# Spreading a weight conversion over two stages of a fused attention and mixture-of-experts kernel

## The chip, the cores and the metric

The kernel runs on one core of one Trainium2 chip. The metric is the time of one execution in device microseconds (us); of several runs the median is given. A profiled execution is one more run, with a trace of every engine: TensorE (PE, its weight loads PEld), VectorE (DVE), ScalarE (ACT), GpSimd (POOL) and SyncE (SP), which here issues most of the loads.

## The reference, cut to what matters

Three stages run one after the other on 2 x 768 tokens: attention in clusters (2 batches, 8 heads, 64 wide), a mixture of 8 experts with one expert for each token, and a dense pair of products with a gate between them.

```
def _moe2_ref(x, w_in, w_out):          # x: 1536 x 512, w_in: 512 x 2048, w_out: 2048 x 512
    h = x @ w_in
    sp = np.where(h > 20.0, h, np.log1p(np.exp(np.minimum(h, 20.0))))
    g = h * np.tanh(sp)
    return g @ w_out

def reference(q, k, v, centroids, moe_..., moe2_w_in, moe2_w_out):
    x = _attn_ref(q, k, v, centroids)   # softmax(q k') v within clusters, per head
    x = _moe_ref(x, ...)                # x -> gate * relu(x @ w1[e]) @ w2[e]
    return _moe2_ref(x, moe2_w_in, moe2_w_out)
```

The weights of the last stage arrive as 64-bit floating-point numbers. The change concerns when they are turned into the pairs of 16-bit numbers that the products use.

## The kernel before, in words

Every operand of a product is a pair of f16 tiles, a high part and a low part (the rounding error), and every product is three matmuls (`mm3`: high x high, high x low, low x high).

**Attention.** `attention()` is a generator that yields 3 times for each of 16 heads x 6 key tiles, and the heads' work is written in its slots: scores s (L389), their exponentials e on ACT, eh and el (the low part is a subtraction on POOL, L115), the products av (L425 to L427), row maxima mxh on DVE (L349, L354), the head's output xt (L440). `pregate` and `gate(b)` compute the experts of a batch (gate for batch 0 inside attention, for batch 1 right after it): about 45 small DVE instructions, the last of them L1175, then a scatter of the tokens to a buffer in device memory on POOL (L800), a load of the sorted tokens xs on SP (L830), and sorting products with diagonal tiles dg (L700, L711), whose result is xw.

**Experts.** `moe1()` walks (batch b, slot s, block n): products eps<-xw,w into hT for n < 4, eps<-hT,w into x for n > 3, 24 matmuls of 416 columns a block. Weights come in blocks wf; ACT makes the high part (L916), DVE the low part (L920).

**The last stage.** `h_units(q)` for six pieces q of 256 tokens: 16 products h (f = 0 to 15, L1005 with win, 12 matmuls each). `mish` turns a group of four into activations (ACT with table loads, L1101 to L1111, DVE L1108, POOL L115). `o_units(q)` multiplies them by wout (L1157), in four groups f4.

**The conversion.** `convs("i")` and `convs("o")` convert w_in into win and w_out into wout in 16 chunks each. A chunk is one load raw on SP (L1017, 512 KB, two buffers), three DVE instructions that put the bits of a 64-bit number together as a 32-bit one (L1025, L1026, L1028, all 128x512 into the one tile f), the high part on ACT (L1031) and the low part on DVE (L1033). So it is four DVE instructions a chunk. The generator yields 6 times after the first two loads and 4 times for each chunk, and issues the load of chunk j + 2 after the third DVE instruction of chunk j. Column block j of win is what h for f = j needs; chunk j of wout is row block j.

**What sets the order.** Generators are advanced in turn, and each advance writes instructions. In attention the loop `for na, _ in enumerate(attention())` advances `CI = convs("i")` in every second slot (CI1 = 2) after slot 162 (NA0), except while batch 0's gate is being sorted; whatever is left of CI is written in one go after attention. Then come three calls of `mix`: it always advances the part that has come least far, measured as its progress over the weight that stands beside it. A part that yields None waits for another. The first call mixes slot (0, 1) of the experts, gate 1, 20 steps of the output conversion (CV1) and h_units(0); the second slot (1, 0), h_units(1) and the rest of the output conversion; the third slot (1, 1) and all of the rest. From this program order a scheduler makes the queues of PE, DVE, ACT and POOL, by a model of the times; each engine then works its queue in order. SP's queue stands as it was written.

Of the kernel before, what the change touches and what calls it, by code (L numbers as in the profile page):

```python
# [24 lines left out]
def clustered_attention_moe_kernel(  # L25
# [35 lines left out]
    GAP = 1  # L61
    AVL = 1
    ASK = 2
    CV1 = 20
    FM = 0.35
    SE = 8
    SM = 3
# [10 lines left out]
    F32H = 8  # L78
    WL = 0
    FAST = 1  # L80
    CI1 = 2
    CQ = 0
    WM = 1
    FLD = 0
# [3 lines left out]
    SPK = 1  # L88
    WQ = 2
    BQ = 0  # L90
    GA = 40.0
    NA0 = 3*6*9
    ROW = 2 * DM + 8

# [914 lines left out]
    NF = DF2 // P  # L1009
# [23 lines left out]
        nc.vector.scalar_tensor_tensor(out=dst[:, 1], in0=ff, scalar=64.0, in1=dst[:, 0], op0=ALU.mult, op1=ALU.subtract)  # L1033

    NCV = 16

    def convs(nm):
        n = (DF2 if nm == "i" else NF) // NCV

        def load(j):  # L1040
            if nm == "i":
                conv_load((nm, j), w_in[:, j * n:(j + 1) * n].rearrange("(c p) f -> p c f", p=P), [CD, n])
            else:
                conv_load((nm, j), w_out[j * n * P:(j + 1) * n * P, :].rearrange("(c p) f -> p c f", p=P), [n, DM])

        for j in range(RAWB):
            load(j)
        for _ in range(6):
            yield 1.0
        for j in range(NCV):  # L1050
            if nm == "i":
                ch = conv_chunk((nm, j), win[:, :, :, j * n:(j + 1) * n], [CD, n])
            else:
                ch = conv_chunk((nm, j), m_p["wout"][:, :, j * n:(j + 1) * n, :], [n, DM])
            next(ch)
            yield 1.0
            next(ch)
            yield 1.0
            next(ch)
            if j + RAWB < NCV:  # L1060
                load(j + RAWB)
            yield 1.0
            for _ in ch:
                pass
            yield 1.0

    QW = S // 3
# [48 lines left out]
    o_done = set()  # L1116
# [3 lines left out]
    def h_units(q):  # L1120
        b, p = divmod(q, 3)
        x1 = x1_t[b]
        while (b, min(p, 1)) not in slots_done:
            yield None
        for f in range(NF):
            while q > 1 and (q - 2, f // 4) not in o_done:
                yield None
            if f % FB == 0:
                h_t[q] = m_p["ps"].tile([P, FB, QW], F32, tag="h", name="h", bufs=2)
            mm3(h_t[q][:, f % FB], win, x1[:, :, :, p * QW:(p + 1) * QW], CD, slice(f * P, (f + 1) * P))  # L1130
            advance()
            if f % FB == 1:
                pend.append(mish(h_t[q], gsl[q % 2][f // FB], q, f // FB))
                next(pend[-1])
            h_keys.add((q, f))
            if q > 1:
                yield 1.28
            elif f % 2:
                yield 2.56
# [4 lines left out]
    def o_units(q):  # L1144
        b, p = divmod(q, 3)
        wout = m_p["wout"]
        pts = [m_p["ps"].tile([P, DM], F32, tag="o", name="o", bufs=NQ) for _ in range(NQ)]
        for f4 in range(NF // 4):
            while (q, 4 * f4 + 3) not in g_done:
                if (q, 4 * f4 + 3) in h_keys:  # L1150
                    advance()
                else:
                    yield None
# [105 lines left out]
    def mix(*parts):  # L1259
        for u in gmix(*parts):  # L1260
            assert u is not None
# [12 lines left out]
    CI = convs("i")  # L1274
# [7 lines left out]
    def m_until(b, s):  # L1282
        while (b, s) not in slots_done:
            yield next(M)
# [25 lines left out]
        m_step()  # L1310
    att.close()
    open_second()
    for _ in CI:
        pass

    def gate1():
        while not gs1.done:
# [5 lines left out]

    C1, CH = 33.6, 20.5
    CV = convs("o")
    mix([m_until(0, 1), 2 * C1 - m_done[0]], [gate1(), GA], [part(CV, CV1), float(CV1)], [h_units(0), CH])
    mix([m_until(1, 0), C1], [h_units(1), CH], [CV, 4.0 * NCV + 6 - CV1])
    ho = seq(*[gmix([h_units(q + 2), CH], [o_units(q), CH]) for q in range(4)], o_units(4), o_units(5))
    mix([m_until(1, 1), C1 / FM], [ho, 10 * CH])
    rest()  # L1330


# [33 lines left out]
```

## Time and profile before

| what | us |
|---|---|
| median of 3 runs (708.71 to 711.01) | 709.72 |
| the profiled execution | 704.72 |
| its span, first to last instruction | 703.1 |
| PE busy in the span | 616.4 (88%) |
| DVE busy | 433.1 (62%) |
| ACT busy | 448.4 (64%) |
| POOL busy | 299.1 (43%) |

The shares are averages over stages with different limits. Attention runs to about 326 us (the last xt), batch 1's gate ends at 352 us, the sorted tokens of batch 1 are there at about 387 us, and from 460 us on PE has no gap up to the last products. The conversion's DVE instructions lie between 217.7 and 453.7 us. A busy PE is not PE at its peak, since the ends of matmuls are modelled.

### The profile page before, as it was taken

What the parts mean: (1) busy time and instruction counts of PE and PEld (TensorE: products, weight loads), DVE (VectorE), ACT (ScalarE), POOL (GpSimd) and SP (SyncE); (2) the same over time, 40 slices, a digit from 0 to 9 for tenths busy, and PEclk for the clock granted to TensorE, in tenths of its full rate; (3) what the DMA queues carried; (4) which work ended last, traced back from release to release, by engine and by line L of the source; (5) the groups of instructions that cost most, each with busy time, mean ns of one, the idle gap of its engine ahead of it and who ended that gap; (6) DMA issues with size and microseconds to landing.
All of it is one profiled execution on the core that took longest, in us unless ns stands there. A gap on an engine that the chain in (4) does not pass through costs nothing.

```text
span 703.1 us, 14009 instructions
## 1 busy us (share of the span) xinstructions
PE 616.4 (88%) x5618; PEld 408.3 (58%) x5619; DVE 433.1 (62%) x783; ACT 448.4 (64%) x668; POOL 299.1 (43%) x252
## 2 busy tenths in 40 slices
PE   1698989976678985888999898999999999999995
PEld 1375767744346653554766565666666676667542
DVE  6888888899999999789948888832311101110100
ACT  2587888876457676565597668856645466766500
POOL 5578797995956665542061211111212212313211
PEclk9999999999689999999999999999999999999999
DMA  7532462413833333245545544421100000000000
GB/s 228 139 73 69 111 167 57 106 42 86 277 108 98 97 96 90 79 134 179 151 167 168 176 150 154 147 61 31 46 16 1 7 24 1 31 1 20 12 31 34
DMA packets 56743, 64.43 MB, mean 92 GB/s; under 512 B 10080, under 2 KB 46944, under 8 KB 56672
## 3 DMA queue, kind: packets, MB, share of 16 engines
q1 hardware_dynamic: 42064, 48.74, 24.3%
q10 hardware_dynamic: 12688, 8.42, 3.9%
q0 software_dynamic: 1920, 6.32, 2.3%
q8 instruction: 46, 0.75, 0.4%
q14 instruction: 25, 0.20, 0.1%
HBM read 46.23 MB, written 6.32 MB: 75 GB/s over the span
## 4 chain that ended last, share of the span: by engine, by line
PE 42%; DVE 32%; issue 9%; ACT 6%; DMA 5%; POOL 2%; SPq 1%; POOLq 0%; DVEq 0%; ACTq 0%
PE h L1005 12%; PE o L1157 12%; PE eps L1005 7%; DVE mxh L349 4%; DVE f L1026 4%; DVE w L920 3%; DVE f L1028 2%; DMA QK<-oT 2%; PE s L389 2%; DVE oT L299 2%; DVE mxh L354 2%; DVE f L1025 2%; DVE win L1033 2%; PE x L348 1%; DMA wf<-in_moe_w_dram 1%
## 5 line engine op out<-in xcount | busy, mean ns | idle before, releaser
L115 POOL TENSOR_TENSOR el<-e,eh 128x768 f16<-128x768 f32 x86 | 146.9, 1718 | 59.3 <-ACT eh L398 35.0
L1005 PE MATMUL h<-x,win 128*128 128x256 f16 x1152 | 133.4, 273 | 4.3 <-ACT s L1101 2.8
L1108 DVE SCALAR_TENSOR_TENSOR s<-s,h 128x1024 f32<-128x1024 f32 x24 | 29.3, 1221 | 167.7 <-ACT s L1106 165.1
L1005 PEld LDWEIGHTS <-win 128*128 128x128 f16 x1152 | 112.5, 98 | 24.5 <-issue 5.1
L1005 PEld LDWEIGHTS <-w 128*128 128x128 f16 x768 | 75.1, 99 | 66.9 <-issue 13.5
L115 POOL TENSOR_TENSOR xb<-s,xb 128x1024 f16<-128x1024 f32 x18 | 39.6, 2201 | 142.9 <-ACT xb L1111 142.7
L1157 PE MATMUL o<-wout,xb 128*128 128x512 f16 x432 | 96.8, 379 | 0.0
L391 ACT ACTIVATE e<-s 128x384 f32<-128x384 f32 x152 | 70.2, 486 | 24.7 <-PE s L389 20.1
L389 PE MATMUL s<-QK 128*128 128x384 f16 x320 | 81.9, 347 | 4.4 <-ACT e L391 4.1
L398 ACT ACTIVATE eh<-e 128x768 f16<-128x768 f32 x88 | 73.9, 845 | 16.8 <-PE av L427 7.7
L1005 PE MATMUL eps<-xw,w 128*128 128x416 f16 x384 | 75.1, 344 | 6.2 <-DVE hT L967 3.2
L1005 PE MATMUL eps<-hT,w 128*128 128x416 f16 x384 | 72.7, 342 | 1.4 <-DVE hT L967 1.4
L1101 ACT ACTIVATE s<-h,cst 128x512 f32<-128x512 f32 x48 | 33.0, 687 | 62.6 <-PE h L1005 62.4
L1157 PEld LDWEIGHTS <-xb 128*128 128x128 f16 x432 | 42.3, 98 | 47.6
L425 PE MATMUL av<-vst,eh 128*128 128x65 f16 x528 | 63.9, 197 | 6.8 <-DVE xt L440 5.4
L349 DVE TENSOR_REDUCE mxh<-x 128x1 f32<-128x512 f32 x96 | 63.6, 674 | 5.1 <-PE x L348 4.8
L427 PE MATMUL av<-vst,el 128*128 128x65 f16 x528 | 61.2, 197 | 5.1 <-POOL el L115 4.6
L426 PE MATMUL av<-vst,eh 128*128 128x64 f16 x528 | 64.0, 199 | 0.0
L425 PEld LDWEIGHTS <-eh 128*128 128x128 f16 x528 | 51.1, 100 | 15.8 <-DVE xt L440 8.0
L427 PEld LDWEIGHTS <-el 128*128 128x128 f16 x528 | 51.1, 102 | 11.9 <-POOL el L115 7.1
L426 PEld LDWEIGHTS <-eh 128*128 128x128 f16 x528 | 51.1, 100 | 3.8 <-issue 0.8
L348 PE MATMUL x<-QK 128*128 128x512 f16 x96 | 40.6, 431 | 12.7 <-DVE mxh L349 6.9
(224 smaller groups left out, 1076.7 us busy)
## 6 DMA issues: line engine op xcount, KB each, us to landing
wf<-in_moe_w_dram ACTq DMA_DIRECT2D x16, 512.0 KB, 4.5
raw<-in_moe_w_in_dram SPq DMA_DIRECT2D x16, 512.0 KB, 3.9
raw<-in_moe_w_out_dram SPq DMA_DIRECT2D x16, 512.0 KB, 4.5
wf<-in_moe_w_dram SPq DMA_DIRECT2D x16, 512.0 KB, 3.7
QK<-hl SPq DMA_DIRECT2D x32, 192.0 KB, 3.1
xs<-dr SPq DMA_DIRECT2D x12, 258.0 KB, 3.6
t<-in_k_dram SPq DMA_DIRECT2D x8, 384.0 KB, 4.4
t<-in_q_dram SPq DMA_DIRECT2D x8, 384.0 KB, 3.6
```

What stands on the lines that cost most here:

```text
L115: nc.gpsimd.tensor_tensor(out=out_, in0=in0, in1=in1, op=ALU.subtract)
L348: nc.tensor.matmul(sp, lhsT=st[:, QA, t * P:(t + 1) * P], rhs=st[:, KA, 0:512], start=True, stop=True)
L349: nc.vector.reduce_max(out=mx_t[i][:, t, 0:1], in_=sp, axis=AX.X)
L389: nc.tensor.matmul(sps[hf][:, 0:HS], lhsT=st[:, KA + a, kt * P:(kt + 1) * P], rhs=st[:, QA + a, hf * HS:(hf + 1) * HS], start=(a == 0), st ...
L391: nc.scalar.activation(out=e32[:, hf * HS:(hf + 1) * HS], in_=sps[hf][:, 0:HS], func=AF.Exp, scale=1.0 / float(D) ** 0.5)
L398: nc.scalar.activation(out=eh, in_=e32, func=AF.Copy)
L425: nc.tensor.matmul(av[:, t, :], lhsT=eh[:, cols], rhs=vs[:, h, 0:NV], start=(kt == 0 and t == 0), stop=False, skip_group_check=True)
L426: nc.tensor.matmul(av[:, t, 0:D], lhsT=eh[:, cols], rhs=vs[:, h, NV:], start=False, stop=False, skip_group_check=True)
L427: nc.tensor.matmul(av[:, t, :], lhsT=el[:, cols], rhs=vs[:, h, 0:NV], start=False, stop=(kt == T - 1), skip_group_check=True)
L1005: nc.tensor.matmul(out_, lhsT=wc[:, a, kk, ms], rhs=mv[:, c, kk, :], start=(i == 0), stop=(i == n - 1))
L1101: nc.scalar.activation(out=s[:, u:u + hf], in_=pt[:, u:u + hf], func=AF.Sigmoid, scale=2.0 ** -17, bias=cst[:, 1:2])
L1157: nc.tensor.matmul(pts[t], lhsT=gsl[q % 2][f // FB][:, f % FB, a, t * P:(t + 1) * P], rhs=wout[:, c, f, :], start=(f == 0 and i_ == 0), st ...
```

## The change

Conversion in attention runs in every fourth slot instead of every second (CI1), and what is left of it is no longer written at once: it goes on in the first `mix`, together with the first 26 steps of the output conversion instead of 20. The first two calls of `mix` become one. The rest of the output conversion, so far in the second call, goes into the last one, with a weight of 5 x 64 beside 205 for h and o. A set cv_done records the chunks that are written; h of block f is not written before chunk f of win, and group f4 of o not before the four chunks of wout that it reads.

```diff
-    CV1 = 20
+    CV1 = 26
-    CI1 = 2
+    CI1 = 4
+    CVF = 5.0
-    GA = 40.0
+    GA = 90.0
     NCV = 16
+    assert NCV == NF
+    cv_done = set()
             for _ in ch:
                 pass
+            cv_done.add((nm, j))
             yield 1.0
         for f in range(NF):
-            while q > 1 and (q - 2, f // 4) not in o_done:
+            while ("i", f) not in cv_done or q > 1 and (q - 2, f // 4) not in o_done:
                 yield None
         for f4 in range(NF // 4):
+            while ("o", 4 * f4 + 3) not in cv_done:
+                yield None
             while (q, 4 * f4 + 3) not in g_done:
     open_second()
-    for _ in CI:
-        pass
+    cv_left = 4.0 * (NCV - sum(k_[0] == "i" for k_ in cv_done))
     C1, CH = 33.6, 20.5
     CV = convs("o")
-    mix([m_until(0, 1), 2 * C1 - m_done[0]], [gate1(), GA], [part(CV, CV1), float(CV1)], [h_units(0), CH])
-    mix([m_until(1, 0), C1], [h_units(1), CH], [CV, 4.0 * NCV + 6 - CV1])
+    mix([seq(m_until(0, 1), m_until(1, 0)), 3 * C1 - m_done[0]], [gate1(), GA], [seq(CI, part(CV, CV1)), cv_left + CV1], [seq(h_units(0), h_units(1)), 2 * CH])
     ho = seq(*[gmix([h_units(q + 2), CH], [o_units(q), CH]) for q in range(4)], o_units(4), o_units(5))
-    mix([m_until(1, 1), C1 / FM], [ho, 10 * CH])
+    mix([m_until(1, 1), C1 / FM], [ho, 10 * CH], [CV, CVF * 4.0 * NCV])
```

Lines of the changed kernel have numbers higher by 1 from there on through the conversion (L1034 for L1033), by 4 in `mish` (L1112 for L1108) and by 6 in `o_units` (L1163 for L1157). The DVE queue between the last head's output and batch 1's gate, before:

```order
L440 TENSOR_TENSOR xt<-av,r 128x384
L989 SCALAR_TENSOR_TENSOR x_4239<-eps,x_4239 128x416
L920 SCALAR_TENSOR_TENSOR w<-wf,w 128x1024
L1033 SCALAR_TENSOR_TENSOR win<-f_5661,win 128x4x128
L967 SCALAR_TENSOR_TENSOR hT<-eps,hT 128x416
L1025 TENSOR_SCALAR f_5669<-raw 128x512
L1026 SCALAR_TENSOR_TENSOR f_5669<-raw,f_5669 128x512
L967 SCALAR_TENSOR_TENSOR hT<-eps,hT 128x416
L471 COPY xT<-x 128x768
L1028 SCALAR_TENSOR_TENSOR f_5669<-raw,f_5669 128x512
L920 SCALAR_TENSOR_TENSOR w<-wf,w 128x1024
```

and after (the gate's first instruction is L728, gmx):

```order
L441 TENSOR_TENSOR xt<-av,r 128x384
L921 SCALAR_TENSOR_TENSOR w<-wf,w 128x1024
L968 SCALAR_TENSOR_TENSOR hT<-eps,hT 128x416 x2
L472 COPY xT<-x 128x768
L921 SCALAR_TENSOR_TENSOR w<-wf,w 128x1024
L968 SCALAR_TENSOR_TENSOR hT<-eps,hT 128x416
L484 SCALAR_TENSOR_TENSOR l<-x,l 128x48
L485 SCALAR_TENSOR_TENSOR l<-x,l 128x48
L968 SCALAR_TENSOR_TENSOR hT<-eps,hT 128x416
L728 TENSOR_REDUCE gmx<-l 128x6
```

No conversion instruction is left between the last xt and the gate's end. In all, 18 chunks stand in front of the gate's last instruction before, and 8 after.

SP's queue from the last scatter of cluster rows (QK<-oT) to the first expert weights of batch 1, before:

```order
L1017 DMA raw<-in_moe_w_in_dram 128x4x128 x12
L1017 DMA raw<-in_moe_w_out_dram 128x512 x2
L830 DMA xs<-dr 128x1032 x2
L1017 DMA raw<-in_moe_w_out_dram 128x512
L830 DMA xs<-dr 128x1032 x4
L1017 DMA raw<-in_moe_w_out_dram 128x512
```

and after:

```order
L1018 DMA raw<-in_moe_w_in_dram 128x4x128 x6
L831 DMA xs<-dr 128x1032 x2
L1018 DMA raw<-in_moe_w_in_dram 128x4x128 x3
L831 DMA xs<-dr 128x1032 x4
L1018 DMA raw<-in_moe_w_in_dram 128x4x128
```

The loads of input chunks 9, 10 and 11 now stand behind the first two loads of batch 1's sorted tokens, and the other four token loads behind chunk 11.

DVE's queue from the third and fourth diagonal tile of batch 1's sorted tokens on (dg, ids and xw belong to these tokens, tm to the experts' output, s to an activation), before:

```order
L700 TENSOR_SCALAR dg<-ident_103,xs 128x128 x2
L856 CAST ids<-xs 128x1
L1025 TENSOR_SCALAR f_6313<-raw 128x512
L989 SCALAR_TENSOR_TENSOR x_4239<-eps,x_4239 128x352
L991 SCALAR_TENSOR_TENSOR tm<-eps,tm 128x64
L1026 SCALAR_TENSOR_TENSOR f_6313<-raw,f_6313 128x512
L920 SCALAR_TENSOR_TENSOR w<-wf,w 128x1024
L1028 SCALAR_TENSOR_TENSOR f_6313<-raw,f_6313 128x512
L718 SCALAR_TENSOR_TENSOR xw<-o,xw 128x4x128 x2
L700 TENSOR_SCALAR dg<-ident_103,xs 128x128 x2
L856 CAST ids<-xs 128x1
L1033 SCALAR_TENSOR_TENSOR wout<-f_6313,wout 128x512
```

and after:

```order
L719 SCALAR_TENSOR_TENSOR xw<-o,xw 128x4x128
L990 SCALAR_TENSOR_TENSOR x_4239<-eps,x_4239 128x352
L992 SCALAR_TENSOR_TENSOR tm<-eps,tm 128x64
L1034 SCALAR_TENSOR_TENSOR win<-f_5960,win 128x4x128
L1026 TENSOR_SCALAR f_6131<-raw 128x512
L1027 SCALAR_TENSOR_TENSOR f_6131<-raw,f_6131 128x512
L1029 SCALAR_TENSOR_TENSOR f_6131<-raw,f_6131 128x512
L701 TENSOR_SCALAR dg<-ident_103,xs 128x128 x2
L857 CAST ids<-xs 128x1
L990 SCALAR_TENSOR_TENSOR x_4239<-eps,x_4239 128x352
L701 TENSOR_SCALAR dg<-ident_103,xs 128x128 x2
L857 CAST ids<-xs 128x1
```

Before, one output chunk (f_6313, wout) is spread over the first six diagonal tiles; after, the whole of input chunk 9 (f_5960, win) and three of the four instructions of chunk 10 (f_6131) stand in front of the fifth.

## Rows read from the trace of the kernel before

**Rows 1.** The page's 40 slices: busy tenths of TensorE and VectorE.
```profile
PE   1698989976678985888999898999999999999995
DVE  6888888899999999789948888832311101110100
```

**Rows 2.** Stretches: length, busy us of each engine (instructions), TensorE's granted clock, DMA share, GB/s.
```profile
50.00:100.00 50.00, 44.68 (x631) 33.76 (x628) 44.37 (x92) 41.17 (x75) 42.48 (x36) 1.00 0.43 113
217.70:283.20 65.50, 50.80 (x601) 33.20 (x597) 65.19 (x100) 44.03 (x79) 38.51 (x25) 0.97 0.30 85
283.20:340.50 57.30, 50.90 (x474) 31.61 (x475) 50.15 (x71) 33.67 (x57) 20.75 (x12) 0.91 0.48 145
217.70:352.20 134.50, 113.40 (x1187) 74.87 (x1184) 126.27 (x221) 85.23 (x147) 59.67 (x38) 0.95 0.38 113
...
328.00:332.00 4.00, 4.00 (x25) 2.11 (x24) 3.38 (x6) 0.67 (x2) 1.19 (x1) 0.64 0.76 234
352.20:412.00 59.80, 54.83 (x420) 37.71 (x419) 43.52 (x79) 44.97 (x62) 17.74 (x14) 1.00 0.54 177
412.00:460.00 48.00, 43.92 (x288) 27.95 (x286) 39.65 (x50) 38.01 (x47) 7.39 (x4) 1.00 0.41 132
460.00:690.00 230.00, 230.00 (x1480) 144.63 (x1479) 33.13 (x37) 128.05 (x142) 47.94 (x31) 1.00 0.06 21
```

**Rows 3.** What TensorE waits for from 217.7 to 352.2: us, times, longest.
```profile
PE x L348 <- DVE mxh L349: 5.0, 4, 3.9
...
PE eps L1005 <- DVE x L989: 2.5, 2, 2.3
```

**Rows 4.** VectorE's instructions on the conversion's tile f alone: stretch, length, busy us.
```profile
217.70:292.80 75.10, 32.49 (x32) 0.95 0.29 82
292.80:352.20 59.40, 34.62 (x40) 0.94 0.50 151
...
352.20:460.00 107.80, 41.72 (x56) 1.00 0.48 157
```

**Rows 5.** Timeline of POOL and VectorE: start, us, instruction, [idle before <-releaser].
```profile
301.02 1.66 POOL L115 TENSOR_TENSOR el<-e,eh 128x768 f16<-128x768 f32 x1 [2.97 <-ACT eh L398]
...
301.21 2.02 DVE L1028 SCALAR_TENSOR_TENSOR f<-raw,f 128x512 int32<-128x512 int32 x1
...
320.76 0.69 DVE L1026 SCALAR_TENSOR_TENSOR f<-raw,f 128x512 int32<-128x512 int32 x1
...
364.73 1.29 DVE L700 TENSOR_SCALAR dg<-ident,xs 128x128 f16<-128x128 f16 x2 [0.90 <-DMA xs<-dr]
...
396.85 2.61 DVE L1026 SCALAR_TENSOR_TENSOR f<-raw,f 128x512 int32<-128x512 int32 x1
```

**Rows 6.** Timeline of TensorE.
```profile
322.73 2.27 PE L1005 MATMUL eps<-xw,w 128*128 128x416 f16 x12 [0.17 <-DVE x L989]
327.34 3.95 PE L1005 MATMUL eps<-xw,w 128*128 128x416 f16 x12 [2.34 <-DVE x L989]
...
366.10 1.50 PE L711 MATMUL o<-dg,xs 128*128 128x128 f16 x24
...
383.64 2.78 PE L1005 MATMUL h<-x,win 128*128 128x256 f16 x24
386.26 4.38 PE L1005 MATMUL eps<-hT,w 128*128 128x416 f16 x24
390.48 1.75 PE L1005 MATMUL eps<-xw,w 128*128 128x416 f16 x9
```

**Rows 7.** Timeline of SyncE's DMA queue: when a load was issued.
```profile
361.99 0.81 SPq L830 DMA_DIRECT2D xs<-dr  x2
362.92 0.36 SPq L1017 DMA_DIRECT2D raw<-in_moe_w_out_dram  x1
366.97 0.99 SPq L830 DMA_DIRECT2D xs<-dr  x2
```

**Rows 8.** VectorE's groups by shape, 352.2 to 460: count, busy us, mean ns, idle before.
```profile
L920 DVE SCALAR_TENSOR_TENSOR w<-wf,w 128x1024 f16<-128x1024 f32 x13 | 16.5, 1272 | 0.2 <-ACT w L916 0.2
...
L1025 DVE TENSOR_SCALAR f<-raw 128x512 int32<-128x512 int32 x14 | 5.9, 422 | 1.2 <-DMA raw<-in_moe_w_out_dram 1.0
```

## The prediction

> **What bounds the kernel now.** I read the page's 40 slices first. VectorE (DVE) is at eight tenths or more in nearly every slice from 8 to 20 and nearly idle from slice 26 on; TensorE (PE) is dented in the first half and full from slice 26 to the end [rows 1]. So there are two kernels in one span: attention with its vector work, bound by DVE, and a tail bound by PE. The stretches say it in numbers [rows 2]. From 217.7 us (the first conversion instruction) to 352.2 us (the last instruction of batch 1's gate) DVE is busy 126.27 of 134.5 us and PE 113.40, so PE stands 21.1 us. From 352.2 to 412 PE stands 59.80 - 54.83 = 5.0 us, from 412 to 460 4.1 us, and from 460 to 690 nothing at all. What PE loses before 460 is all that the change can win; after 460 nothing gives it back, and nothing absorbs a delay.
>
> Who stops PE in the first stretch is in the waits [rows 3]: the row maxima and the expert output's low half, both DVE. And DVE is full there with the conversion: 32.49 us for the first 32 conversion instructions and 34.62 us for the next 40 [rows 4]. Four of them make a chunk, so these 67.1 us are 18 chunks, 16 of the input and 2 of the output weights; 14 more follow up to 460, for 41.72 us.
>
> **Part 1, conversion taken out of attention.** The order of DVE before and after shows how many chunks go: 18 in front of the gate's last instruction become 8. These eight keep nearly the places of the first eight; ten are gone from the stretch, 34.62 us of DVE [rows 4]. That is more than PE can use: against 126.3 - 34.6 = 91.7 us of DVE stand 113.4 of PE. So PE becomes the bound, and the gain is PE's idle time there, not DVE's saving. PE's work up to the gate's products hardly changes (276 expert products and 36 h in place of 271 and 49, 32 of them pulled ahead of attention's end), and nothing is added to any engine there, which excludes a loss. By sections [rows 2]:
>
> - 217.7 to 283.2: four conversion instructions of 26 leave. DVE is busy 65.19 of 65.5 us, so what is taken out shortens it: one chunk, 32.49 / 8 = 4.1 us. Bounds 0 and 4.1 us; I take 3.0, near the upper end since DVE has no gap.
> - 283.2 to 352.2: the other 36 go from here. PE stands 57.30 - 50.90 = 6.4 us up to 340.5 and not at all behind it. Bounds 0 and 6.4; I take half, 3.2, because attention without any conversion, 50 to 100 us, also leaves PE idle 5.3 of 50 us [rows 2].
> - The clock. PE's granted clock is 0.91 from 283.2 to 340.5 [rows 2]. [...] The work lost is busy time by what the clock lacks of 1: 50.90 x 0.09 = 4.6 us. The wait of 2.34 us is for DVE and should go; I take 1.5, bounds 0 and 4.6.
>
> Sum of part 1: 3.0 + 3.2 + 1.5 = 7.7 us won, bounds 0 and 15.1.
>
> A chunk is dear in attention for a second reason. L1028 takes 2.02 us while GpSimd (POOL) subtracts 128x768, and L1026 0.69 us where no such work stands beside it [rows 5]; a chunk is 4.1 us in the first row and 41.72 / 14 = 2.98 us in the last [rows 4]. [...] The row's price for ten moved chunks is 29.8 us with these collisions; four undisturbed instructions, 0.42 + 3 x 0.69 = 2.49 us a chunk [rows 5, 8], would make it 24.9.
>
> **Part 2, the chunks that now come late.** Eight input chunks move behind the gate, and the products h of chunk f may be written only once chunk f is. In the new order SP loads chunks 9, 10 and 11 behind two loads of sorted tokens, which wait for the scatter: in the trace those go out at 361.99 and the load behind them, an output chunk, at 362.92 [rows 7]. Up to PE's first sorting product at 366.10 the new order gives PE about what the old one did (36 + 24 h and 12 + 16 + 29 expert products in place of 47 + 24 + 7 and 17 + 29), so nothing changes there. From then on both engines can be added up to chunk 16. PE: 128 expert products at 4.22 / 24 = 0.176 us (386.26 to 390.48), 144 h at 2.62 / 24 = 0.109 us (383.64 to 386.26), 72 sorting products in 3 x 1.50 us, together 42.7 us [rows 6]. DVE, from the first diagonal at 364.7 [rows 5]: 8 x 2.49 = 19.9 us of conversion undisturbed and 27.1 us of other work (twelve diagonals, the low halves of six expert weights, of six hT and of seven pieces of sorted tokens, two activations, small ones, each at its mean over 352.2 to 460, as 1.27 us for an expert weight [rows 8]), 47.0 us. PE could be through at 408.8, DVE not before 411.7: DVE stays the bound here. Where it is the bound it has been busy 99% (217.7 to 283.2), and between 352.2 and 412, where it is not, 43.52 / 59.80 = 73% [rows 2]. I take 93%: 50.5 us, chunk 16 at 415.2, PE idle 6.4 us in place of 5.0, so 1.5 us lost. Bounds: 5.0 us won (all idle time of 352.2 to 412 gone), 15.3 us lost (73%: 64.4 us, chunk 16 at 429.1, 20.3 us idle less 5.0).
>
> What is queued behind the new waits: on PE everything, since h stands among the expert products; on DVE hT and x, for which PE waits; on SP the last four loads of sorted tokens, now behind the load of chunk 11, which needs the buffer of chunk 9, and expert weights behind loads of chunks. Those token loads went out at 366.97 [rows 7], now hardly before chunk 9 is through L1028, some five us later. Their cover is the 40 expert products that stand between the second and the third pair of tiles, 7.0 us; without it the five us come on top.
>
> **Part 3, the output weights.** All sixteen chunks now come behind the input's last; counted behind the gate it is 24 chunks of both kinds in place of 14. DVE needs 66.8 us for them (39.8 us of conversion, 27.0 of other work between), and it is busy only 33.13 of 230 us after 460 [rows 2], so the ten chunks' 24.9 us fit in. I take 0; bounds 4.1 us won (the idle time of 412 to 460) and 5 us lost, two chunks' time. Ten ScalarE halves of the conversion move along with their chunks, two table loads go, and the gate's share in the mix is scaled with the mix: costed at nothing, since ScalarE is busy 44.97 of 59.80 us where they arrive [rows 2].
>
> **The sum.** 7.7 - 1.5 - 0 = 6.2 us. The profiled execution takes 704.72 us (its span 703.1), so 698.5 for one like it; the runs shown have a median of 709.72, 5.0 us above it. From that median: 703.5 us.
>
> **Rivals.** (a) PE gets nearly all of it: 11 us in part 1, 3 in part 2, 709.7 - 14 = 696 us. For it: DVE's saving is over one and a half times PE's idle time. Against: PE stands 11% without any conversion, too. (b) Displaced: part 1 wins 7.7 and chunks 9 to 16 cost as much, 709.7 us. For it: DVE's work is only moved, and the full PE behind 460 gives nothing back. (c) Slower: DVE keeps its 73% up to chunk 16, because each chunk hands its tile to ScalarE and back and stands behind activations that wait for ScalarE's tables; chunk 16 at 429.1, 709.7 + 15.3 - 7.7 = 717.3 us. It decides below a busy share of 47.0 / 56.8 = 83%, where the loss is 7.7. For it: h had full cover and now waits; against: in the old order nobody hurried these instructions. (d) The clock: eight waits on chunks as long as that of 2.34 us, each followed by 3.95 - 2.27 = 1.7 us of lost work [rows 6], 13.4 us: 703.5 + 13.4 = 716.9 us. Against: from 352.2 to 460 PE waits too, and its granted clock stays 1.00 [rows 2]. [...]
>
> **Chances.** Forecast 54% (698 to 708 us), (a) 16%, (b) 14%, (c) 12%, (d) 4%. About 0.3% (2.1 us) is what a measurement of this kernel can tell from no change: faster means under 707.6. Nearly all of the forecast and (a) is faster, 66%; (b) and the forecast's upper edge are the same, 18%; (c) and (d) are slower, 16%. For 8 in 10 the range reaches from the lower side of (a), 694.5, over (b) to halfway between (b) and (c), 712.5.
>
> **What would show it.** Right: the gate's last instruction 6 to 9 us before 352.2 with eight chunks ahead of it and PE idle under 14 us up to it; then chunk 16 about 63 us behind it, PE's waits on win 5 to 8 us in all, none on wout, and the last o as far ahead as the gate less 1 or 2 us. Wrong: waits on win of 15 us or more or granted clocks below 0.9 behind the gate, or a PE that stands over 16 us in front of it.

## The result, and the profile after

The changed kernel takes 697.78 us (median of 4 runs, 697.22 to 699.62) against 709.93 us before: a ratio of 0.983, 95% interval 0.981 to 0.986. In a second measurement it took 699.39 us against 708.23, 0.988 (0.984 to 0.992). So it wins 9 to 12 us; 6.2 were forecast. One execution of the kernel before that took 3424.25 us is left out of all that follows. The profiled executions differ by less: 699.62 and 704.72 us, spans of 697.9 and 703.1.

In the order of the rows of before, here are the busy tenths of the page [rows 1]:

```profile
PE   1597989978679995999988889899999999999995
...
DVE  6879887999899999736469888688321110110100
```

VectorE's full block now ends at slice 15 (counted from 0) and comes back at slices 21 to 27: the conversion has moved. For the account, the program is cut at four instructions that every kernel of this study has: the output xt of the eleventh head (heads counted from 1), that of the fourteenth, the last instruction of batch 1's gate, and 500 us. The columns are those of [rows 2]: length, busy us of PE, its weight loads, DVE, ACT and POOL (instructions), TensorE's granted clock, DMA share, GB/s. Before:

```profile
216.64:283.17 66.53, 51.86 (x618) 34.00 (x616) 66.22 (x102) 45.07 (x81) 39.16 (x26) 0.97 0.29 84
283.17:352.15 68.98, 62.55 (x586) 41.62 (x587) 61.06 (x123) 41.15 (x68) 21.12 (x13) 0.93 0.46 138
352.15:500.00 147.85, 138.80 (x970) 91.41 (x968) 93.73 (x139) 105.42 (x134) 31.68 (x21) 1.00 0.40 129
```

and after:

```profile
218.69:278.80 60.11, 49.05 (x614) 32.71 (x612) 59.41 (x99) 42.68 (x76) 37.55 (x25) 1.00 0.36 102
278.80:339.02 60.22, 58.54 (x577) 39.34 (x577) 35.61 (x87) 37.57 (x62) 21.41 (x14) 0.97 0.26 80
339.02:500.00 160.98, 145.97 (x1016) 95.83 (x1015) 118.55 (x178) 112.80 (x147) 33.88 (x21) 1.00 0.48 153
```

PE's idle time is length less busy. Ahead of the gate's end it falls from 14.7 + 6.4 to 11.1 + 1.7 us, 8.4 less; behind it, it rises from 9.0 to 15.0, 6.0 more. The third term is in the busy columns: from the eleventh head's output to the end PE is busy 448.1 us before and 443.5 after, for the same products. These 4.6 us are put down to the clock; the granted clocks of the rows give nearly as much: 0.03 x 51.86 + 0.07 x 62.55 = 5.9 us lacking up to the gate before, 0.03 x 58.54 = 1.8 after, 4.2 less (rows at 1.00 and 0.99 left out). With 0.2 us at the end the account is 8.4 - 6.0 + 4.6 + 0.2 = 7.2 us; measured from the eleventh head's output to the end it is 486.5 - 479.2 = 7.3. What comes ahead of that output is not touched by the change and took 216.6 us in the one profile and 218.7 in the other (215.3 to 220.3 in all profiles of this study); this is why the spans differ by 5.2.

The rest, up to 9 or 12 us, is in how the executions differ. Those of the kernel before lie between 702.9 and 711.7 us, and the profiled one, 704.72, is among the quick ones; those of the changed kernel lie between 697.2 and 700.4. The mean granted clock was 0.962 and 0.960 over 18 and 28 executions of before, and 0.971 in the profiled one; of the changed kernel 0.971 and 0.969 over four each, and 0.971 in both profiled ones. The clock is only a part of it: over those 18 and 28 executions of before, time and mean clock go together loosely (correlation -0.35 and -0.36, a slope of about 1.7 us for a hundredth), so a hundredth of clock explains less than 2 us. The rest stays open.

Behind the gate TensorE waits like this (engine, line waited for, us in all, times, longest; [rows 3] has the other side of the gate):

```profile
PE h L1006 <- ACT s L1105: 8.9, 6, 2.0
PE h L1006 <- DVE s L1112: 2.6, 2, 1.8
PE h L1006 <- ACT win L1032: 1.5, 1, 1.5
PE o L712 <- DVE dg L701: 1.4, 1, 1.4
PE o L1163 <- DVE wout L1034: 0.3, 1, 0.3
```

On win itself PE waits once, for 1.5 us. It waits for the activations, L1105, six times. One such wait shows where that comes from. First TensorE, then ScalarE just ahead of it:

```profile
372.03 1.14 PE L1006 MATMUL h<-x,win 128*128 128x256 f16 x9 [2.00 <-ACT s L1105]
```

```profile
368.81 0.63 ACT L1032 ACTIVATE win<-f 128x512 f16<-128x512 f32 x1 [2.20 <-DVE f L1029]
369.35 0.64 ACT L716 ACTIVATE xw<-o 128x128 f16<-128x128 f32 x2
370.00 1.28 ACT L1105 ACT_TABLE_LOAD   x1
371.30 0.69 ACT L1105 ACTIVATE s<-h,cst 128x512 f32<-128x512 f32 x1
```

ScalarE stood 2.20 us for VectorE's third step of a chunk (L1029), since the chunk's high half was next in its queue; the table load and the activation stand behind it in the queue, and TensorE stood 2.00 us for the activation. The same pair stands again at 393.46 on ScalarE (2.14 us) and at 397.09 on TensorE (1.24 us). Behind 400 us the same shows with output chunks: ScalarE stood 3.20 us at 421.61 and 2.19 at 433.28, TensorE 1.73 at 428.33 and 1.86 at 440.51. But these waits of ScalarE are no measure of what TensorE loses. Here they are, from the gate to 500 us, for the changed kernel (two lines), the kernel before, and flush, which is explained below:

```profile
ACT wout L1032 <- DVE f L1029: 23.1, 11, 4.1
ACT win L1032 <- DVE f L1029: 6.7, 4, 2.2
ACT wout L1031 <- DVE f L1028: 21.1, 10, 4.4
ACT wout L1032 <- DVE f L1029: 22.1, 10, 3.1
```

TensorE's waits for activations beside them are 8.9, 2.8 and 2.0 us. ScalarE waits for output chunks in all three; by the author's reading it costs TensorE only where an activation that it needs stands right behind. That the hand-on makes up all of the 8.9 us is argued from such rows, not shown by a run.

### The profile page after: what moved, and what is told of

Read it like the earlier page. It is cut to its first block, busy times and chain, and to the rows that moved or that the text cites. A ratio compares the mean times of both kernels' runs of the same rounds, so it can differ in the third digit from the quotient of the medians.

```text
span 697.9 us, 13994 instructions
## 1 busy us (share of the span) xinstructions
PE 610.3 (87%) x5618; PEld 406.1 (58%) x5619; DVE 426.1 (61%) x783; ACT 446.9 (64%) x666; POOL 299.2 (43%) x252
## 4 chain that ended last, share of the span: by engine, by line
PE 41%; DVE 26%; issue 10%; ACT 9%; DMA 8%; POOL 2%; SPq 2%; POOLq 0%; DVEq 0%; ACTq 0%
PE h L1006 10%; PE o L1163 9%; PE eps L1006 8%; DVE mxh L350 3%; PE s L390 3%; DVE f L1027 3%; DMA wf<-in_moe_w_dram 2%; DVE w L921 2%; DVE f L1029 2%; DMA QK<-oT 2%; DVE f L1026 2%; DMA raw<-in_moe_w_in_dram 2%; DVE mxh L355 2%; DVE oT L300 2%; PE eps L275 1%
## 5 line engine op out<-in xcount | busy, mean ns | idle before, releaser
L1112 DVE SCALAR_TENSOR_TENSOR s<-s,h 128x1024 f32<-128x1024 f32 x24 | 29.3, 1221 | 147.8 <-ACT s L1110 147.8
L116 POOL TENSOR_TENSOR xb<-s,xb 128x1024 f16<-128x1024 f32 x18 | 40.5, 2248 | 167.4 <-ACT xb L1115 167.3
L1163 PE MATMUL o<-wout,xb 128*128 128x512 f16 x432 | 96.7, 379 | 0.0
L1006 PE MATMUL eps<-xw,w 128*128 128x416 f16 x384 | 73.4, 339 | 1.1 <-DVE l L485 0.6
L1163 PEld LDWEIGHTS <-xb 128*128 128x128 f16 x432 | 42.3, 98 | 47.7
L1105 ACT ACTIVATE s<-h,cst 128x512 f32<-128x512 f32 x48 | 32.8, 685 | 56.3 <-PE h L1006 56.0
L428 PE MATMUL av<-vst,el 128*128 128x65 f16 x528 | 61.1, 196 | 4.4 <-POOL el L116 4.4
L921 DVE SCALAR_TENSOR_TENSOR w<-wf,w 128x1024 f16<-128x1024 f32 x32 | 51.7, 1617 | 6.4 <-ACT w L917 6.4
```

The costliest lines, as they stand in the source:

```text
L116: nc.gpsimd.tensor_tensor(out=out_, in0=in0, in1=in1, op=ALU.subtract)
L428: nc.tensor.matmul(av[:, t, :], lhsT=el[:, cols], rhs=vs[:, h, 0:NV], start=False, stop=(kt == T - 1), skip_group_check=True)
L921: nc.vector.scalar_tensor_tensor(out=hl_[:, 1], in0=f, scalar=32.0, in1=hl_[:, 0], op0=ALU.mult, op1=ALU.subtract)
L1006: nc.tensor.matmul(out_, lhsT=wc[:, a, kk, ms], rhs=mv[:, c, kk, :], start=(i == 0), stop=(i == n - 1))
L1105: nc.scalar.activation(out=s[:, u:u + hf], in_=pt[:, u:u + hf], func=AF.Sigmoid, scale=2.0 ** -17, bias=cst[:, 1:2])
L1163: nc.tensor.matmul(pts[t], lhsT=gsl[q % 2][f // FB][:, f % FB, a, t * P:(t + 1) * P], rhs=wout[:, c, f, :], start=(f == 0 and i_ == 0), st ...
```

## The experiments

The table has every run: the ratio of the timed runs to the kernel before, and from the profile the length of heads 12 to 14, PE's idle time from the eleventh head's output to the gate's end and from there to 500 us, and the time from the eleventh head's output to the end. Some expectations count heads from 0: their "heads 11 to 13" are these heads 12 to 14. The profiles of out_only (700.55 us) and thin_only (700.2) are the quickest of their executions, 5.0 and 3.7 us below the medians, so their profile columns flatter them. Medians of different measurements are best compared by their ratios, since the kernel before itself had medians from 706.45 to 709.93 us.

| kernel | median us | ratio (95%) | heads 12-14 | idle ahead | idle behind | to the end |
|---|---|---|---|---|---|---|
| before, first profile | 709.93 | | 66.5 | 21.1 | 9.0 | 486.5 |
| before, again | 707.05 | 0.998 (0.996-1.001) | 66.9 | 21.9 | 7.6 | 486.3 |
| changed, first profile | 697.78 | 0.983 (0.981-0.986) | 60.1 | 12.7 | 15.0 | 479.2 |
| changed, again | 699.39 | 0.988 (0.984-0.992) | 60.4 | 12.2 | 14.5 | 478.6 |
| flush | 696.38 | 0.985 (0.979-0.991) | 60.0 | 16.7 | 6.4 | 475.7 |
| in_only | 712.40 | 1.006 (1.003-1.009) | 59.9 | 12.3 | 19.1 | 490.3 |
| out_only | 705.55 | 0.997 (0.995-0.999) | 66.6 | 20.2 | 8.1 | 483.6 |
| merge_only | 708.54 | 1.000 (0.998-1.003) | 67.1 | 22.1 | 8.1 | 487.7 |
| cvmove_only | 702.92 | 0.992 (0.989-0.994) | 70.3 | 21.4 | 5.6 | 484.1 |
| ci2 | 707.03 | 0.996 (0.994-0.999) | 70.5 | 18.7 | 7.9 | 488.2 |
| thin_only | 703.87 | 0.995 (0.993-0.998) | 60.0 | 17.8 | 9.8 | 480.7 |
| thin_cvmove | 702.75 | 0.996 (0.993-0.999) | 61.1 | 17.7 | 9.5 | 480.5 |
| flush_late | 696.11 | 0.986 (0.982-0.990) | 54.9 | 16.8 | 6.4 | 475.9 |
| flush_ga40 | 702.99 | 0.991 (0.987-0.994) | 61.5 | 16.4 | 11.2 | 483.4 |

**Both kernels again.** Nothing is edited.

> The kernel before once more, against itself. The changed kernel won 12.1 us by the medians, but the two profiled executions differ by 5.2 us of span only (703.1 and 697.9 us), and its own profile of before was 5 us below its other executions. Theory A (the gain is in the traces, the rest is spread between executions): ratio 1.000 within 0.3%, and a second profile whose span lies anywhere from 703 to 709 us, its difference to the first spread over the stretch ahead of 217 us, which the change doesn't touch. Theory B (executions without a profiler run another way): the second profile is again near 703 us while the timed executions stay near 709.7 us.

> The changed kernel once more. Ratio 0.983 plus or minus 0.003 in either theory. Theory A: a span near 696 us, batch 1's gate done near 339 us and chunk 16 some 61 us behind it, as in the first profile; less time ahead of 218 us than there. Theory B: again a span near 698 us.

Both readings of the gap between timed and profiled executions had a miss. The second profile of before spans 704.2 us, and its difference to the first is spread (1.3 us of it ahead of the eleventh head's output); its executions lie between 704.0 and 708.6. The changed kernel's profile was again 697.9. So nothing speaks for a profiler's effect; the kernel before simply varies more from one execution to the next.

**The ten chunks put back ahead of the gate** (flush). This is the test of the prediction's main part.

```diff
     open_second()
+    for _ in CI:
+        pass
     cv_left = 4.0 * (NCV - sum(k_[0] == "i" for k_ in cv_done))
```

> The changed kernel with one thing undone: what is left of the input conversion when attention ends is again converted in one go, so that 18 chunks stand ahead of the gate's last instruction as before the change; the output conversion and the merged mix stay as changed. Theory 1 (the gain comes from the ten chunks that left the stretch ahead of the gate): the gate is done near 352 us again, PE idle there near 21 us, the time 707 to 712 us, no gain. Rival 2 (the gain comes from behind the gate: the merged mix and the output conversion spread into the outputs): the time stays at 697 to 701 us.

The first theory fell at once: 18 chunks stand ahead of the gate, it is done at 355.26 us, and the kernel takes 696.4 us.

```profile
219.94:279.97 60.03, 49.03 (x612) 32.80 (x610) 59.50 (x99) 42.67 (x76) 37.48 (x25) 0.99 0.35 102
279.97:355.26 75.29, 69.55 (x639) 45.72 (x637) 67.76 (x131) 49.92 (x79) 24.49 (x15) 0.96 0.45 137
355.26:500.00 144.74, 138.38 (x974) 91.99 (x973) 94.44 (x137) 105.35 (x134) 32.87 (x19) 1.00 0.41 132
```

Beside the rows of after: with the chunks ahead of the gate PE stands 5.7 instead of 1.7 us there, and 6.4 instead of 15.0 behind it. Taking ten chunks out of that stretch brought the gate 15 us forward (counted from the eleventh head's output) and won nothing; the idle time went behind the gate and grew by 4.6 us in all. (In the medians of one measurement flush is 3.0 us ahead of the changed kernel, but the intervals of the two ratios overlap, so neither is shown to be the faster.)

**The input part alone** (in_only). CI1 = 4 and the deferred chunks as changed; the mixes and the output conversion as before, but the gate's share still 90:

```diff
-    CV1 = 26
+    CV1 = 20
-    mix([seq(m_until(0, 1), m_until(1, 0)), 3 * C1 - m_done[0]], [gate1(), GA], [seq(CI, part(CV, CV1)), cv_left + CV1], [seq(h_units(0), h_units(1)), 2 * CH])
+    mix([m_until(0, 1), 2 * C1 - m_done[0]], [gate1(), GA], [seq(CI, part(CV, CV1)), cv_left + CV1], [h_units(0), CH])
+    mix([m_until(1, 0), C1], [h_units(1), CH], [CV, 4.0 * NCV + 6 - CV1])
-    mix([m_until(1, 1), C1 / FM], [ho, 10 * CH], [CV, CVF * 4.0 * NCV])
+    mix([m_until(1, 1), C1 / FM], [ho, 10 * CH])
```

> The input part alone: conversion thinned in attention and the rest behind it as changed, but the output conversion, its weight (20 steps) and the two first mixes as before the change. Theory 1: 8 chunks ahead of the gate, gate done near 339 us, PE idle near 13 us ahead of it; behind it DVE is fuller (24 chunks before the third mix), so 698 to 704 us. Rival 2: the output part is what wins, so 706 to 711 us.

Ahead of the gate all is as in the changed kernel (gate done at 340.25, 12.3 us idle), and yet it takes 712.4 us, more than before and above both expectations. Its stretch from the gate to 500 us, and the waits in it:

```profile
340.25:500.00 159.75, 140.64 (x934) 89.03 (x933) 115.93 (x176) 109.02 (x140) 30.71 (x19) 0.96 0.47 149
```

```profile
PE h L1006 <- ACT s L1105: 5.8, 4, 2.5
PE h L1006 <- DVE s L1112: 3.0, 2, 2.5
PE h L1006 <- ACT win L1032: 2.9, 2, 2.4
PE eps L1006 <- ACT w L917: 2.7, 1, 2.7
```

PE stands 19.1 us there, and the granted clock is 0.96 where it is 1.00 in the changed kernel. With the output conversion left in this stretch, the eight deferred input chunks cost more than all that was won ahead of it. One place in the stretch:

```profile
376.33 3.04 PE L1006 MATMUL h<-x,win 128*128 128x256 f16 x12 [2.39 <-ACT win L1032]
```

Twelve products h take 3.04 us behind that wait, where 24 take 2.62 at a granted clock of 1.00 [rows 2, 6]; from 340.25 to 400 the granted clock is 0.94.

**The output part alone, and its halves** (out_only, merge_only, cvmove_only). All three have the input conversion as before (CI1 = 2, the rest in one go, GA = 40). out_only then has the changed mixes; merge_only has the merged mix with the whole output conversion in it; cvmove_only keeps two mixes and puts the rest of the output conversion into the third:

```diff
 # merge_only
+    mix([seq(m_until(0, 1), m_until(1, 0)), 3 * C1 - m_done[0]], [gate1(), GA], [CV, 4.0 * NCV + 6], [seq(h_units(0), h_units(1)), 2 * CH])
+    mix([m_until(1, 1), C1 / FM], [ho, 10 * CH])
 # cvmove_only, CV1 = 20
+    mix([m_until(0, 1), 2 * C1 - m_done[0]], [gate1(), GA], [part(CV, CV1), float(CV1)], [h_units(0), CH])
+    mix([m_until(1, 0), C1], [h_units(1), CH])
     mix([m_until(1, 1), C1 / FM], [ho, 10 * CH], [CV, CVF * 4.0 * NCV])
```

> The output part alone: the input conversion as before the change (every second slot, the rest in one go after attention, the gate's share 40), the two first mixes merged and the output conversion beside the outputs as changed. The first theory (gain ahead of the gate) fell with the run that kept 18 chunks there and took 696.4 us. Theory 3 (the whole net gain comes from the output part): 696 to 700 us, and from head 11's output to the last instruction 476 to 480 us instead of 486.4. Theory 4 (thinning in attention is half of it): 702 to 705 us and 481 to 484 us.

> One half of the output part alone: the first two mixes merged, so that h of piece 1 can fill gaps of TensorE earlier, but the whole output conversion stays in that merged mix, ahead of the outputs; the input conversion as before the change. Theory 3a (the merged mix wins by giving TensorE work for its gaps): 697 to 702 us. Theory 3b (the output conversion's place wins, since VectorE is crowded up to 460 us): 706 to 711 us.

> The other half alone: the two first mixes stay apart as before the change and 20 steps of the output conversion stay in the first, but the rest of it goes from the second into the third, beside the outputs; the input conversion as before the change. Theory 3a (the merged mix wins): 706 to 711 us. Theory 3b (the output conversion's place wins): 697 to 702 us, with TensorE idle under 5 us between 352 and 460 us instead of 9.

The output part is not the whole gain: 705.6 us, half a microsecond beyond theory 4's range (its 483.6 us to the end lie inside). Merging alone does nothing (708.5). Moving the output conversion is worth 6 us by itself (702.9, just outside theory 3b's 697 to 702); PE's idle time behind the gate falls from 9.0 to 5.6 us. With the two together, 705.6: the parts don't add.

**Conversion in attention back to every second slot** (ci2). One number of the changed kernel:

```diff
-    CI1 = 4
+    CI1 = 2
```

> The changed kernel with conversion in attention in every second slot again; the rest of it still behind attention and not in one go. 12 input chunks stand ahead of the gate's last instruction instead of 8, 4 behind it instead of 8. Theory of displacement (a chunk ahead of the gate costs about what it costs behind it, and behind it a little more): the gate 5 to 7 us later than in the changed kernel, the time 697 to 699.5 us, between the 699.4 of 8 chunks and the 696.4 of 18. Rival (the late chunks cost nothing and the two differ by chance): 699 to 706 us, growing with the gate's delay.

Neither expectation had this: 707.0 us, 7.6 more than the changed kernel in its second measurement. 12 chunks stand ahead of the gate, and PE stands 7.9 us behind it instead of 15.0; the loss is in heads 12 to 14 and at the end.

```profile
218.27:288.72 70.45, 57.34 (x633) 37.37 (x631) 67.72 (x103) 46.31 (x82) 38.71 (x26) 0.88 0.28 80
```

These three heads take 70.45 us instead of 60.11, at a granted clock of 0.88 instead of 1.00; TensorE is busy 57.34 us for 633 matmuls against 49.05 for 614. Over all profiles of the study, the six of kernels with every second slot from the start have 66.5 to 70.5 us in these heads and clocks from 0.97 down to 0.88; the seven with every fourth slot have 59.9 to 61.5 us and clocks from 0.96 to 1.00. In all six, 26 conversion instructions lie in these heads, in all seven 22. That four instructions shorten the heads by more than their own time has a second part. VectorE's busy time there falls by 6.8 us (66.22 and 59.41), but only 3.1 of that is conversion. The rest comes from instructions that both kernels have. Before:

```profile
L363 DVE TENSOR_SCALAR m<-mx 128x12 f16<-128x12 f32 x3 | 4.0, 1336 | 0.0
L290 DVE TENSOR_TENSOR seq<-seq,desc 128x192 f32<-128x192 f32 x2 | 2.7, 1333 | 0.0
L865 DVE TENSOR_TENSOR xw<-xw,gmask 128x512 f16<-128x512 f16 x2 | 2.0, 976 | 0.0
L293 DVE TENSOR_TENSOR seq<-seq,smx 128x192 f32<-128x192 f32 x2 | 1.5, 768 | 0.0
```

and after:

```profile
L364 DVE TENSOR_SCALAR m<-mx 128x12 f16<-128x12 f32 x3 | 2.2, 721 | 0.1
L291 DVE TENSOR_TENSOR seq<-seq,desc 128x192 f32<-128x192 f32 x2 | 1.4, 717 | 0.0
L866 DVE TENSOR_TENSOR xw<-xw,gmask 128x512 f16<-128x512 f16 x2 | 0.8, 412 | 0.0
L294 DVE TENSOR_TENSOR seq<-seq,smx 128x192 f32<-128x192 f32 x2 | 0.7, 345 | 0.0
```

The stretched ones, seven of the nine before (0.88 to 1.61 us, where the others take 0.34 and 0.41) and three after (0.89 to 1.11), begin while an instruction of GpSimd runs: the third m<-mx took 1.51 us beside a subtraction before, and 0.17 us beside nothing after. VectorE's time on everything but the conversion is 39.0 to 40.5 us in the six profiles and 35.2 to 36.5 in the seven. Which instructions collide is a matter of the order, and no run tests it by itself.

**Thinning alone, and with the output conversion moved** (thin_only, thin_cvmove). The first is the kernel before, the second cvmove_only, each with this one edit:

```diff
-    CI1 = 2
+    CI1 = 4
```

> The kernel before with one number changed: conversion in attention in every fourth slot instead of every second (CI1 = 4), the rest of the input conversion in one go behind attention and the output conversion as before the change. 18 chunks stand ahead of the gate as before the change; only some five conversion instructions leave the three heads up to head 14's output. Theory 5 (these heads, where VectorE is full, are the larger part of the gain, as 699.4 against 707.0 us with CI1 = 4 and 2 in the changed kernel says): 700 to 703 us, heads 11 to 13 in 60 us instead of 66.5 and the clock 0.98 or more in them. Theory 6 (thinning wins only together with the other parts): 706 to 710 us.

> CI1 = 4 and the rest of the output conversion moved beside the outputs, and nothing else of the change: the input conversion's rest in one go behind attention, the two first mixes apart, the gate's share 40. Theory 5 with parts that add: the 702.9 us of the moved output conversion less 7 to 9 us of the thinning, 694 to 697 us, faster than the changed kernel. If the deferred chunks or the merged mix are needed for the gain (theory 6): 699 us or more.

Thinning alone gives 703.9 us, 0.995, a microsecond beyond theory 5's range. The place is the expected one:

```profile
217.82:277.81 59.99, 49.20 (x612) 32.62 (x610) 59.41 (x99) 42.68 (x76) 37.44 (x25) 1.00 0.35 102
```

The heads take 60.0 instead of 66.5 us, and 5.7 of these 6.5 reach the end (480.7 against 486.4). The times of the executions show about half of it. On top of the moved output conversion it gives nothing: 702.8 against 702.9 us. There its heads take 61.1 instead of 70.3 us, but PE stands 9.5 instead of 5.6 us behind the gate. Theory 6 was nearer here. So the one number CI1 was changed in four surroundings: it won in three (the kernel before; out_only, below; ci2) and nothing in the fourth.

**Conversion later in attention** (flush_late). On flush:

```diff
-    CI1 = 4
+    CI1 = 2
-    NA0 = 3*6*9
+    NA0 = 252
```

> As the kernel with the rest of the input conversion in one go (696.4 us), but conversion in attention begins only at slot 252 and then runs in every second slot: up to heads 12, 13, 14 and 15 there are 0, 1, 3 and 7 chunks done instead of 0, 2, 5 and 8. If VectorE is what binds heads 11 to 14, they take 3 to 5 us less and the time is 692 to 695 us; if the conversion there has stopped costing anything once the clock is steady, 696 to 698 us.

```profile
218.41:273.32 54.91, 48.91 (x613) 33.21 (x611) 51.88 (x91) 41.07 (x73) 33.19 (x24) 0.97 0.32 93
273.32:356.19 82.87, 72.04 (x658) 47.34 (x658) 71.99 (x134) 54.38 (x86) 33.09 (x21) 0.96 0.48 151
```

The heads get 5.1 us shorter still and PE's idle time in them falls from 11.0 to 6.0, as VectorE's bound says (busy 51.88 of 54.91 us); in the next stretch it rises from 5.7 to 10.8. The time is that of flush, 696.1 us: displaced once more.

**The gate's share back to 40** (flush_ga40). On flush; it is also out_only with CI1 = 4.

```diff
-    GA = 90.0
+    GA = 40.0
```

> The kernel with the rest of the input conversion in one go (696.4 us, 0.985 of before) with the gate's share at 40 again; it is at the same time the output part alone (705.6 us, 0.997) with conversion in attention in every fourth slot. So it stands one number away from each. Theory 7 (thinning's price is that of the three heads, 6 to 7 us, whatever else is changed): 697 to 700 us, 0.984 to 0.989 of before, heads 11 to 13 in 60 us; the gate's share is then worth little. Theory 8 (the gate's larger share is what makes thinning and the merged mix add up): 701 to 705 us, 0.992 to 0.997, with more idle time of TensorE behind head 13 than the 14.4 us of the kernel with 90.

703.0 us, as theory 8 expected. Against out_only it shows what the thinning is worth, 0.997 to 0.991. Against flush it is that of the share, and the profile has it behind the gate:

```profile
355.46:500.00 144.54, 133.39 (x934) 88.87 (x933) 88.52 (x135) 99.56 (x128) 30.65 (x19) 0.99 0.40 130
```

11.2 us idle instead of 6.4, with 934 matmuls done instead of 974; from the fourteenth head on it is 16.9 us against 12.1 (the 14.4 of the expectation was a miscount). The share changes the order of h among the expert products, and the wait for activations is 5.2 us instead of 2.0:

```profile
PE h L1006 <- ACT s L1105: 5.2, 4, 2.6
PE h L1006 <- ACT s L1105: 2.0, 3, 1.0
```

The profiles differ by 7.7 us to the end, the ratios by some 4 us, and the two ratios' intervals overlap (0.979 to 0.991 and 0.987 to 0.994), so what the share is worth is likely rather than shown.

**Taken together.** Take one part out of the changed kernel: without the thinning it is 707.0 us (ci2), without the output part 712.4 (in_only), without the deferred chunks 696.4 (flush). The first two are needed for the gain, the third is not. (in_only keeps the gate's share of 90 in a mix that had 40 before the change, so a part of its loss can be that.)

## Why the prediction was right and where it was wrong

The direction and the range of 8 in 10 held; the size was half to two thirds. The time came 0.2 us below the forecast's own band of 698 to 708 us in the first measurement and inside it in the second, near rival (a)'s 696 us, though not on its way. The reason that carried most of the text did not hold, and the sum came near by errors that cancel: the first three terms won 5.2 us more than forecast, the last two lost 4.5 us more. By the prediction's own terms, in us won:

| term | forecast | measured |
|---|---|---|
| idle time of PE, 217.7 to 283.2 | 3.0 | 3.6 |
| idle time of PE up to the gate | 3.2 | 4.7 |
| clock | 1.5 | 4.6 |
| part 2, gate to chunk 16 | -1.5 | -2.3 |
| part 3, output weights | 0 | -3.7 |
| sum | 6.2 | 6.9 |

(Part 2 is the 7.3 us that PE stands from 339 to chunk 16 at 400 against 5.0 in the 60 us behind the gate before; part 3 is the rest of the 6.0 that the idle time behind the gate grew by. The 0.2 us at the end and rounding make up the difference to 7.2.)

- **What held.** Eight chunks ahead of the gate, PE idle 12.7 us there (forecast: under 14), and chunk 16 done 61.6 us behind the gate's last instruction (forecast: 63). From the first diagonal tile to the end of chunk 16 VectorE was busy 42.92 of 47.73 us, 90% (forecast: 93%), and PE idle 6.2 us (forecast: 6.4). The token loads: the last four went out 10.6 us behind the first two instead of 5.0 us [rows 7], and no wait of PE came of it.

```profile
352.90:400.63 47.73, 41.56 (x324) 28.38 (x325) 42.92 (x81) 27.56 (x44) 8.77 (x6) 1.00 0.58 180
```

```profile
350.11 0.81 SPq L831 DMA_DIRECT2D xs<-dr  x2
351.04 9.58 SPq L1018 DMA_DIRECT2D raw<-in_moe_w_in_dram  x3
360.72 6.43 SPq L831 DMA_DIRECT2D xs<-dr  x4
```

- **Signs that failed.** The gate's last instruction came 13.1 us before 352.2, not 6 to 9. PE's waits on win are 1.5 us, not 5 to 8. The end came 7.3 us earlier and the gate 15.2 (both counted from the eleventh head's output), 7.9 us apart, not 1 or 2: about half of what was won ahead of the gate was lost again behind it.
- **Collisions with POOL.** The moved chunks cost about what they did before in this place [rows 4]: 51.52 / 69 x 4 = 2.99 us each up to 460, as the row's price said, and 17.05 / 27 x 4 = 2.53 beyond, near the 2.49 of four undisturbed instructions. The trace shows collisions in the new place too: between the gate and 520 us six conversion instructions take 1.45 to 2.50 us where they take 0.42 to 0.70 otherwise, all six begin during a POOL subtraction, and all lie before 460. (One of them, L1026 at 389.74 with 2.24 us, reads only raw; the other five read two tiles.)

```profile
339.30:460.00 120.70, 51.52 (x69) 1.00 0.52 164
460.00:520.00 60.00, 17.05 (x27) 1.00 0.28 85
```

- **The clock was mis-sized.** It was read from one execution, 1.5 us of at most 4.6, and from the stretch behind 283 us alone. The 1.5 us take the slow products at 327.34 [rows 6] as an effect of the wait ahead of them, which no run shows by itself: behind a wait of 2.00 us at 372.03 in the changed kernel nine products h take 1.14 us, behind one of 2.39 us at 376.33 in in_only twelve take 3.04 us. That the measured 4.6 equals the upper bound is chance: by the granted clocks 2.6 us of it are in that stretch and 1.6 in the three heads, for which nothing was set down. In those heads the second profile of before has 0.95 and two other kernels with every second slot have 0.88, where the first has 0.97. Whether this makes the whole gain, 9 to 12 us, larger than the two profiles' 7.3 is not shown.
- **Part 1 hung on the wrong chunks.** It counted the 36 instructions behind 283 us for most of the saving. flush keeps them there and is as fast, and in_only takes them out and is slower than before. What pays in attention is the thinning of the three heads, where four conversion instructions leave (26 become 22) and 6.4 us go; the forecast gave them 3.0 us and at most 4.1, one chunk's time, since it priced only the conversion and not what other VectorE instructions lose beside it. The idle time that the other chunks leave ahead of the gate comes back behind it. That was rival (b), and for this half of the change it is the true one.
- **Parts 2 and 3, the deferral.** Part 3 was costed at nothing because VectorE has room behind 460 us. The room is there (VectorE is busy 49.45 us from 460 to 690 after), but TensorE doesn't wait for wout (0.3 us); it waits for ScalarE's activations (8.9 us). The ScalarE halves that move along were "costed at nothing, since ScalarE is busy 44.97 of 59.80 us"; that term failed by 3.7 us, and a share of busy time could not show what stands behind a wait in ScalarE's queue (the 2.20 us at 368.81). In part 2 the size was nearly right, but there too the waits were expected on win and came from the activations. It isn't the place of the output conversion that costs this: moved alone, it won 6 us (cvmove_only). It is the ten deferred chunks ahead of it: with them PE stands 15.0 us behind the gate, without them 6.4 (flush). Their price is 8.6 us, forecast 1.5, and the cut at chunk 16 in the table hides a part of it under part 3. That ScalarE's queue is what makes them dear is read from the rows, and no run tests it alone.
- **The gate's share** was costed at nothing too; flush_ga40 points to 4 us or more.

What stays open: why thinning and the moved output conversion don't add, what the gate's share is worth beyond the touching intervals, and what makes executions of one kernel differ by 9 us. The order that the scheduler makes changes with every edit, so effects of 3 us and less can't be put down to the edit alone here.

## What to carry to other kernels

Where two engines are both nearly full, taking work from one stretch can move the idle time to another (changed against flush, PE stands 4.0 us less ahead of the gate's end and 8.6 us more behind it); look for the few instructions in the place where the chain is tightest, and test a move by putting it back alone. Follow a moved step through every queue that it stands in, also that of an engine with time to spare: a wait there can be handed on to whatever is queued behind (ScalarE's 2.20 us at 368.81, TensorE's 2.00 us at 372.03). Price a move by all that gets shorter or longer beside it, not by the moved instructions alone (VectorE's busy time in heads 12 to 14 fell by 6.8 us, 3.1 of them conversion). And take several profiles of the kernel before, since one execution can hide what the others lose (704.72 us here, beside a median of 709.93).

## What the runs showed of the hardware

The granted clock in the same stretch of the same program differs between executions: the first profile of before has 0.97 in heads 12 to 14 and the second 0.95. Two other kernels with conversion in every second slot have 0.88, with about 5 us more of busy time (57.3 us for 633 matmuls, 51.9 for 618). The kernels with four conversion instructions fewer in these heads (every fourth slot) had 0.96 to 1.00, in seven profiles of seven.

Small VectorE instructions were stretched beside GpSimd's work as the large ones were (L1027 took 2.50 us at 430.02 and 0.69 at 423.81 in the profile of after): m<-mx of 128x12 took 0.17 us beside nothing and 1.51 us beside a subtraction of 128x768 (profiles of after and before). Not every one was: xw<-xw,gmask at 221.33 in the profile of after took its usual 0.41 us, though such a subtraction began 0.04 us ahead of it.
